# Dividing a gate-and-up tile over two blocks of the 23rd and 24th attention units, in place of the last down tile

## The chip, the cores and the metric

The kernel runs on one NeuronCore of a Trainium2 chip. The metric is the device time of one execution in microseconds (us). Before the change three runs took 1396.32, 1397.09 and 1397.90 us; their median is 1397.09 us. "TensorE" or PE is the matmul engine, PEld its weight loads, ScalarE or ACT the activation engine, VectorE or DVE the elementwise engine, GpSimd or POOL and SyncE or SP the two others; SP and POOL issue most DMAs.

## What is computed

A layer norm of 2048 tokens of 512 features feeds an attention of 32 heads of 16 features, and beside it a SwiGLU feed-forward of width 1792, whose output gates the attention's:

```python
xn = _layernorm(x, axis=-1)
s = _A_ref(xn, A_wqkv, A_wo)        # softmax(q k' / 4) v, 32 heads of 16, then @ wo
g = _silu(_B_ref(xn, B_w_gate, B_w_up, B_w_down))   # (silu(xn@w_gate) * (xn@w_up)) @ w_down
return x + s * g
```

Shapes: x is [1, 2048, 512], `wqkv` [512, 1536], `wo` [512, 512], `w_gate` and `w_up` [512, 1792], `w_down` [1792, 512], all float32.

## The kernel before

**Units and blocks.** After a prologue (layer norm, projections to q, k, v) attention runs in 32 *units*: 8 groups of 4 heads times 4 batches of 512 queries (`units`, line 463). A unit goes over its 2048 keys in 16 *key tiles* of 128. It is cut into three *blocks* of 4 to 6 key tiles, so there are 96 blocks, numbered 0 to 95 here; unit *u*, counted from 0, has blocks 3*u* to 3*u*+2. The 23rd and 24th units are thus blocks 66 to 71, the 29th and 30th are blocks 84 to 89. `run(u, first, n)` (line 963) issues one block of *n* key tiles.

**What a block does.** It has 2*n* *score pairs*: for each key tile two pairs of heads, each pair two matmuls that run side by side on the two halves of TensorE's rows. Most pairs are *direct* (`scored`, line 950): they go into one of two double banks `score0` and `score1`, and ScalarE's exponential (line 954) reads the bank and writes a `pr` tile. The others are *copied* (lines 1001 to 1017): they go half by half into the spare bank `acc1`, VectorE copies them out, and ScalarE takes their exponential in place afterwards (line 1024). At the end come the *values*: for each key tile eight matmuls (line 409) that multiply `pr` by v into `acc0`, for all 128 rows of TensorE.

**The fillers.** While ScalarE works through the scores, TensorE is given other work, in *filler pairs*: two matmuls, again one on each half of the rows, into `bankx` and `banky` (`both`, line 185, and lines 379 to 380). They come from generators in a queue: `ffn(b)` for the four batches of tokens, then the output projections `project_out`. A feed-forward batch has two groups of 7 gate-and-up tiles (24 pairs each) followed by 4 down tiles (21 pairs each). At the end of a gate-and-up tile ScalarE takes a tanh of `bankx` (line 239) and VectorE makes the hidden tile from both banks (lines 240 to 241); at the end of a down tile of the second group VectorE adds the banks to `y` and ScalarE takes a tanh of `y` (line 191).

**How many fillers a block gets** stands in the list `sizes` (lines 483 to 492), one number a block, and so one tile a block. There are 88 feed-forward tiles, of which the first is done in the prologue, and the projections make 8 entries more; that is 95 for 96 blocks. One tile is therefore divided over two blocks. Before the change it is the last down tile: 11 pairs in block 86 and 10 in block 87. Block 88 (`early`) has the first part of the projection (18 pairs), block 89 and those after it 24 each, but 12 in blocks 92 and 93.

**Order within a block.** `events(n, f, ahead)` (line 511) sets how many pairs are direct and lays direct scores (D), halves of copied ones (A, B) and fillers (F) out in a row. VectorE's other work waits in the list `chores` and is let in between the copies where it has room. What a unit leaves to do when its values are complete (`finish`, line 437: transposing `acc0`, scaling) joins that list behind the first two scores of the next unit.

**Begun blocks.** Where the next block's number is in `begins` (line 493), `run` issues the next block's first two direct scores ahead of the last key tile's values (lines 1031 to 1034), so that ScalarE has work during them. Before, blocks 86, 87, 88, 92 and 93 are begun in this way. Lines 496 to 509 set the number of key tiles: 4, 6, 6 or 6, 6, 4 in the last four units, elsewhere 5, 5, 5 with one more in one block.

**The end of the feed-forward.** After each down tile of the last batch `next_out` (line 284) splits a piece of `wo` and of the attention output for the projection, and loads the next piece of `wo` into one buffer (`wor`). Block 88 needs the first three of them, block 89 the fourth.

Of the kernel before, what the change touches and what calls it, by code (L numbers as in the profile page):

```python
# [39 lines left out]
DC = D // HALF  # L40
# [3 lines left out]
EPS = 1e-5  # L44
TURNS = (0, 0, 0, 0, 0, 2, 4, 6, 8, 10, 13, 16, 16)
COPIES = ((0, 0, 0, 1, 1, 1, 1, 0, 0, 0, 0, 2), (1, 1, 0, 0, 1, 1, 1, 1, 2, 2, 0, 0))
QSLOT = (0, 1, 0)
KSLOT = (0, 0, 1)

# [2 lines left out]
def tile_block(ctx: ExitStack, tc: tile.TileContext, x, wqkv, wo, w_gate, w_up, w_down, out):  # L52
# [42 lines left out]
    def load_rows(dst, src, slots):  # L95
        for h in range(2):
            for s, part in enumerate(slots):
                r = h * HALF + 2 + s * DH
                sp.dma_start(dst[r:r + DH].bitcast(F32),
                             src[part].rearrange("(j h d) t -> h d j t", j=2, h=2)[h])  # L100
# [5 lines left out]
    def load_q(u, i=None):  # L106
        g, b = divmod(u, NB)
        load_rows(qst[u % 2 if i is None else i], q_d[:, g * 64:(g + 1) * 64, b * TB:(b + 1) * TB], QSLOT)

# [353 lines left out]
    units = NG * NB  # L463
# [19 lines left out]
    sizes = []  # L483
    for _ in range(NB):
        for part in GROUPS:
            nf = part.stop - part.start
            sizes += [3 * DC] * nf + [3 * nf] * NT
    split = sizes[-1] // 2
    sizes = sizes[1:-1] + [sizes[-1] - split, split]
    early = len(sizes)  # L490
    pair = 6 * DT
    sizes += [6 * (DT - 1), pair, pair, pair, pair // 2, pair // 2, pair, pair]
    begins = (early - 2, early - 1, early, early + 4, early + 5)

    blocks, opened = [], []
    for u in range(units):
        opened.append(len(blocks))
        if u == 0:
            ns = [4, 6, 6]
        elif u >= units - 4:  # L500
            ns = ([4, 6, 6] if u % 2 else [6, 6, 4])
        else:
            ns = [5] * 3
            far = sizes[len(blocks):len(blocks) + 3]
            ns[far.index(max(far)) if far[1] < max(far) else 1] = 6
        kt = 0
        for n in ns:
            blocks.append((u, kt, n))
            kt += n
# [23 lines left out]
    with ExitStack() as pro:  # L533
# [119 lines left out]
        def split_x(b, t, av, between=None):  # L653
            hi, lo = (xt[b % 2][j][:, :, t * P:(t + 1) * P] for j in range(2))
            nc.scalar.copy(hi, av)
            if between:
                between()
            dve.tensor_sub(lo, av, hi.bitcast(F32))
# [119 lines left out]
        def copy_fx(i):  # L778
            i, w = divmod(i, 2)
            i, u = divmod(i, 2)  # L780
            j, h = divmod(i, 2)
            dst = fx[halves[h], j].rearrange("p (c u) t -> u p c t", u=2)[u]
            nc.scalar.copy(dst[:, 2 * w:2 * w + 2], xt[0][j][halves[u], 2 * w:2 * w + 2])
# [13 lines left out]
        for b in range(NB):  # L797
# [3 lines left out]
            for n, (make, i) in enumerate(slots):  # L801
# [27 lines left out]
                if b == 0 and n == 2:  # L829
                    split_x(0, 0, xf)  # L830
                for _ in range(COPIES[b][n] if b < 2 else 0):
                    copy_fx(copied.pop(0))
# [57 lines left out]
        with tc.If(fast < 1):  # L890
            with tc.tile_pool(name="gen", bufs=1) as gen:
                for h in range(2):
                    pool.memset(qst[0][h * HALF:h * HALF + 2].bitcast(F32), 0.0)
                for g in range(NG):
                    for b in range(NB):
                        u = g * NB + b
# [244 lines left out]
```

## Time and profile before

| what | value |
| --- | --- |
| median of three runs | 1397.09 us |
| the profiled execution's own time | 1397.09 us |
| its span, first to last instruction | 1395.3 us |
| TensorE matmuls busy | 1387.7 us, 99% of the span |
| weight loads busy | 849.8 us, 61% |
| ScalarE busy | 1087.4 us, 78% |
| VectorE busy | 755.9 us, 54% |
| mean DMA rate | 106 GB/s |

The profile is one execution. "Busy" adds up the time in which at least one instruction of an engine is running; matmuls overlap in the pipeline, so 99% for TensorE doesn't say that it runs as densely as it can. In a row of the trace's list in order of time, the first number is the start, the second the length, both in us; instructions of one kind that follow each other are merged ("x48" is 48 matmuls), and what stands in brackets is the engine's idle time before it and what ended it. The 8 matmuls of each key tile at line 409 make these rows a ruler: a block ends where its last row of values ends, which is start plus length.

### The profile page before, as it was taken

To read this page: it belongs to the slowest core of one execution; us is meant where nothing else is said; L and a number is where in the kernel's file an instruction comes from. 1 tells how busy PE (TensorE), PEld (TensorE's weight loads), DVE (VectorE), ACT (ScalarE), POOL (GpSimd) and SP (SyncE) were. 2 spreads that over 40 slices of the span, in tenths; PEclk is the share of its full clock that TensorE was granted. 3 is DMA by queue.
4 is the path that set the end of the run, shared out by engine and by line. 5 is a ranking of instruction groups with operands and counts; after the bars stand their busy time and mean duration, and the time that the engine had idled before them with its cause. 6 is when DMAs were issued, how large, how long until landed. Compare 5 with 4: busy or idle time off the path is not lost.

```text
span 1395.3 us, 27643 instructions
## 1 busy us (share of the span) xinstructions
PE 1387.7 (99%) x11193; PEld 849.8 (61%) x11193; DVE 755.9 (54%) x1293; ACT 1087.4 (78%) x1245; POOL 73.7 (5%) x92
## 2 busy tenths in 40 slices
PE   9999999999999999999999999999999999999998
PEld 7777755655665565565556556655655665564555
DVE  6674555455645653556456645654565445555544
ACT  6753678877888877787888778778877877889785
POOL 4200200000000000000000000000000000000222
PEclk9999999999999999999999999999999999999999
DMA  7778641043534511154514303256134113234323
GB/s 228 271 246 267 173 107 43 14 115 85 130 86 118 119 43 36 51 132 97 136 53 110 97 13 73 74 141 149 57 76 114 32 47 80 63 92 141 116 86 137
DMA packets 126953, 148.13 MB, mean 106 GB/s; under 512 B 12524, under 2 KB 79340, under 8 KB 126052
## 3 DMA queue, kind: packets, MB, share of 16 engines
q1 hardware_dynamic: 121620, 125.79, 34.8%
q0 software_dynamic: 4912, 20.12, 3.9%
q8 instruction: 89, 1.46, 0.4%
q14 instruction: 44, 0.36, 0.1%
q10 hardware_dynamic: 288, 0.39, 0.1%
HBM read 106.68 MB, written 39.58 MB: 105 GB/s over the span
## 4 chain that ended last, share of the span: by engine, by line
PE 88%; ACT 0%; DVE 0%; issue 0%; DVEq 0%
PE acc L409 32%; PE bankx L187 23%; PE score L948 17%; PE banky L187 10%; PE acc L948 3%; PE bankx L380 2%; PE banky L380 1%; ACT pr L954 0%; PE acc L1078 0%; PE bankx L1078 0%; PE score L1078 0%; DVE pr L1010 0%; DVE y L1085 0%; DVE pr L1016 0%; DVE fx L1022 0%
## 5 line engine op out<-in xcount | busy, mean ns | idle before, releaser
L954 ACT ACTIVATE pr<-score 128x1024 f32<-128x1024 f32 x860 | 813.4, 1032 | 226.2 <-PE score L948 224.5
L409 PE MATMUL acc<-pr,vst 128*17 128x512 f32 x4096 | 459.1, 593 | 0.0
L948 PE MATMUL score<-qst,kst 50*128 50x512 f32 x1720 | 395.4, 412 | 0.1
L187 PE MATMUL bankx<-fx,guh 64*128 64x512 f32 x896 | 333.5, 393 | 0.1
L187 PE MATMUL banky<-fx,guh 64*128 64x512 f32 x896 | 324.9, 393 | 0.0
L409 PEld LDWEIGHTS acc<-pr,vst 128*17 128x17 f32 x4096 | 109.9, 97 | 290.6 <-issue 270.9
L948 PEld LDWEIGHTS score<-qst,kst 50*128 50x128 f32 x1720 | 176.3, 184 | 142.5 <-issue 66.3
L1010 DVE COPY pr<-acc 128x512 f32<-128x512 f32 x164 | 113.3, 691 | 188.1 <-PE acc L948 186.0
L187 PE MATMUL bankx<-wd,hh 64*128 64x512 f32 x672 | 201.2, 392 | 0.0
L187 PE MATMUL banky<-wd,hh 64*128 64x512 f32 x672 | 198.8, 393 | 0.0
L187 PEld LDWEIGHTS bankx<-fx,guh 64*128 64x128 f32 x896 | 166.6, 186 | 18.4 <-issue 0.9
L187 PE MATMUL banky<-fx,gul 64*128 64x512 f32 x448 | 175.6, 392 | 0.0
L187 PE MATMUL bankx<-fx,gul 64*128 64x512 f32 x448 | 175.4, 392 | 0.0
L187 PEld LDWEIGHTS banky<-fx,guh 64*128 64x128 f32 x896 | 166.5, 186 | 5.5
L1024 ACT ACTIVATE pr<-pr 128x1024 f32<-128x1024 f32 x164 | 168.0, 1078 | 0.0
L1016 DVE COPY pr<-acc 128x512 f32<-128x512 f32 x164 | 113.3, 691 | 74.9 <-PE acc L948 65.9
L240 DVE SCALAR_TENSOR_TENSOR ga<-th,bankx 128x512 f32<-128x512 f32 x56 | 38.5, 688 | 177.9 <-ACT th L239 177.9
L187 PEld LDWEIGHTS bankx<-wd,hh 64*128 64x128 f32 x672 | 124.9, 186 | 14.2 <-DVE fx L1022 0.8
L948 PE MATMUL acc<-qst,kst 50*128 50x512 f32 x328 | 131.9, 402 | 0.1
L187 PEld LDWEIGHTS banky<-wd,hh 64*128 64x128 f32 x672 | 124.5, 186 | 3.5
L187 PEld LDWEIGHTS bankx<-fx,gul 64*128 64x128 f32 x448 | 83.7, 187 | 9.9
L187 PEld LDWEIGHTS banky<-fx,gul 64*128 64x128 f32 x448 | 83.6, 186 | 3.2
(186 smaller groups left out, 1296.3 us busy)
## 6 DMA issues: line engine op xcount, KB each, us to landing
gur<-in_B_w_gate_dram SPq DMA_DIRECT2D x56, 256.0 KB
gur<-in_B_w_up_dram SPq DMA_DIRECT2D x56, 256.0 KB
wdr<-in_B_w_down_dram SPq DMA_DIRECT2D x56, 256.0 KB
kst<-k_d SPq DMA_DIRECT2D x192, 64.0 KB
qst<-q_d SPq DMA_DIRECT2D x192, 64.0 KB
fx<-xt_d SPq DMA_DIRECT2D x24, 512.0 KB
q_d<-parts SPq DMA_DIRECT2D x16, 512.0 KB
k_d<-parts SPq DMA_DIRECT2D x16, 512.0 KB
```

Of the source, the lines that this page charges most:

```text
L187: mm(banks[i], lhs[halves[i]], rhs[halves[i]], start=start, stop=stop)
L240: dve.scalar_tensor_tensor(ga, th, 1.0, bankx, op0=ALU.add, op1=ALU.mult)
L380: mm(banks[k], lhs[b, c][a][halves[h], (j + k) * P:(j + k + 1) * P], fx[halves[h], w, c], start=swap == i == 0, stop=i == 3 * n - 1, skip_ ...
L409: mm(acc[0][h * 32:h * 32 + DH + 1], v[:, kt % CT, h * (DH + 1):(h + 1) * (DH + 1)], probs[kt, h // 2][:, h % 2], start=kt == 0, stop=kt = ...
L948: mm(bank, k[r, j, kc * P:(kc + 1) * P], qst[u % 2][r, j], start=True, stop=True)
L954: act(pr, score[slot], AF.Exp, scale=0.25)
L1010: dve.tensor_copy(probs[kt, j][:, 0], spare_bank)
L1016: dve.tensor_copy(probs[kt, j][:, 1], spare_bank)
L1024: act(probs[kt, j], probs[kt, j], AF.Exp, scale=0.25)
```

## The change

One table entry is added and three rules of the plan are written anew. Nothing else differs; all lines behind the first stand one line lower.

```diff
+PARTED = (22, 23)
...
-    split = sizes[-1] // 2
-    sizes = sizes[1:-1] + [sizes[-1] - split, split]
+    sizes = sizes[1:]
+    sizes[3 * PARTED[0] + 2:3 * PARTED[1]] = [3 * DC // 2] * 2
     early = len(sizes)
     pair = 6 * DT
     sizes += [6 * (DT - 1), pair, pair, pair, pair // 2, pair // 2, pair, pair]
-    begins = (early - 2, early - 1, early, early + 4, early + 5)
+    begins = tuple(3 * u + i for a in (PARTED[0], units - 2) for u, i in ((a, 2), (a + 1, 0)))
 
     blocks, opened = [], []
     for u in range(units):
         opened.append(len(blocks))
         if u == 0:
             ns = [4, 6, 6]
-        elif u >= units - 4:
+        elif u in PARTED or u >= units - 2:
             ns = ([4, 6, 6] if u % 2 else [6, 6, 4])
         else:
             ns = [5] * 3
```

The gate-and-up tile that block 68 had whole is now 12 pairs in block 68 and 12 in block 69. Every tile behind it comes one block later, up to the last down tile, which block 87 now has whole. Blocks 68, 69, 92 and 93 are begun; 86, 87 and 88 no longer are. By the plan:

| block | before: key tiles, fillers, begun | after: key tiles, fillers, begun |
| --- | --- | --- |
| 66, 67, 68 (23rd unit) | 5, 24 / 6, 24 / 5, 24 | 6, 24 / 6, 24 / 4, 12, begun |
| 69, 70, 71 (24th) | 5, 24 / 6, 24 / 5, 24 | 4, 12, begun / 6, 24 / 6, 24 |
| 72, 73, 74 | 5, 21 / 6, 21 / 5, 21 | 6, 24 / 5, 21 / 5, 21 |
| 75, 76, 77 | 5, 21 / 6, 24 / 5, 24 | 5, 21 / 5, 21 / 6, 24 |
| 78, 79, 80 | 5, 24 / 6, 24 / 5, 24 | 5, 24 / 6, 24 / 5, 24 |
| 81, 82, 83 | 5, 24 / 6, 24 / 5, 21 | 5, 24 / 6, 24 / 5, 24 |
| 84, 85, 86 (29th) | 6, 21 / 6, 21 / 4, 11, begun | 5, 21 / 6, 21 / 5, 21 |
| 87, 88, 89 (30th) | 4, 10, begun / 6, 18, begun / 6, 24 | 5, 21 / 5, 18 / 6, 24 |

In the 29th and 30th units this makes 21+21+21 and 21+18+24 filler pairs, 63 in each, where it was 53 and 52.

**TensorE, the end of block 68 and the start of block 69.** `acc_80` is `acc0`, where the values go, `acc_81` the spare bank; a row "x2" is one pair of scores. Before:

```order
L187 MATMUL bankx<-fx,gul 128x512
L187 MATMUL banky<-fx,gul 128x512
L409 MATMUL acc_80<-pr,vst_8976 17x512 x4
L409 MATMUL acc_80<-pr,vst_8980 17x512 x16
L948 MATMUL score_8970<-qst_8987,kst_549 128x512 x2
L948 MATMUL score_8971<-qst_8987,kst_549 128x512 x2
L187 MATMUL bankx<-fx,guh 128x512
L187 MATMUL banky<-fx,guh 128x512
L948 MATMUL acc_81<-qst_8987,kst_553 128x512
```

After:

```order
L188 MATMUL bankx<-fx,gul 128x512
L188 MATMUL banky<-fx,gul 128x512
L949 MATMUL score_8970<-qst_557,kst_8979 128x512 x2
L410 MATMUL acc_80<-pr,vst_8980 17x512 x12
L949 MATMUL score_8970<-qst_8987,kst_549 128x512 x2
L949 MATMUL score_8971<-qst_8987,kst_549 128x512 x2
L410 MATMUL acc_80<-pr,vst_8980 17x512 x4
L188 MATMUL bankx<-fx,guh 128x512
L188 MATMUL banky<-fx,guh 128x512
L949 MATMUL score_8970<-qst_8987,kst_549 128x512 x2
```

The next unit's first two score pairs now stand ahead of the last key tile's values, and the fillers behind them go on with the same gate-and-up tile.

**TensorE, the end of block 87 and the start of block 88**, where the projection begins (line 380). Before:

```order
L948 MATMUL score_8970<-qst_8987,kst_8979 128x512 x2
L409 MATMUL acc_80<-pr,vst_8980 17x512 x12
L948 MATMUL score_8970<-qst_8987,kst_8983 128x512 x2
L948 MATMUL score_8971<-qst_8987,kst_8983 128x512 x2
L409 MATMUL acc_80<-pr,vst_8980 17x512 x4
L380 MATMUL bankx<-fx,part 128x512
L380 MATMUL banky<-fx,part 128x512
L948 MATMUL score_8970<-qst_8987,kst_8983 128x512 x2
L948 MATMUL acc_81<-qst_8987,kst_549 128x512
```

After:

```order
L188 MATMUL bankx<-wd,hh 128x512
L188 MATMUL banky<-wd,hh 128x512
L410 MATMUL acc_80<-pr,vst_8980 17x512 x16
L410 MATMUL acc_80<-pr,vst_8984 17x512 x4
L949 MATMUL score_8970<-qst_8987,kst_8983 128x512 x2
L949 MATMUL score_8971<-qst_8987,kst_8983 128x512 x2
L381 MATMUL bankx<-fx,part 128x512
L381 MATMUL banky<-fx,part 128x512
L949 MATMUL acc_81<-qst_8987,kst_549 128x512
```

Block 88's first two score pairs now stand behind all of block 87's values.

**VectorE from the end of block 85 (before) or 86 (after) into block 87.** `fx<-wor` and `part<-pair` are `next_out`'s splits, `o<-acc_80` the transposition that frees the value bank. Before:

```order
L1022 CAST fx<-wor 128x512
L1010 COPY pr<-acc_81 128x512
L1016 COPY pr<-acc_81 128x512
L1022 TENSOR_TENSOR fx<-wor,fx 128x512
L1022 CAST part<-pair 128x512
L1022 TENSOR_TENSOR part<-pair,part 128x512
L420 STREAM_TRANSPOSE o<-acc_80 128x512
L425 RECIPROCAL rl<-o 128x16
L1010 COPY pr<-acc_81 128x512
```

After:

```order
L1023 CAST fx<-wor 128x512
L1023 TENSOR_TENSOR fx<-wor,fx 128x512
L1011 COPY pr<-acc_81 128x512
L1023 CAST part<-pair 128x512
L1017 COPY pr<-acc_81 128x512
L1023 TENSOR_TENSOR part<-pair,part 128x512
L1011 COPY pr<-acc_81 128x512
L421 STREAM_TRANSPOSE o<-acc_80 128x512
L426 RECIPROCAL rl<-o 128x16
```

The third `next_out` (first row here) has moved from block 86 into block 87, the transposition still stands behind it, with three copies in between where there were two.

## The prediction

> **What bounds the kernel now.** I read the page first, then the list in order of time, where the rows of values mark the blocks, then the waits of the blocks that change.
>
> ```profile
> span 1395.3 us, 27643 instructions
> PE 1387.7 (99%) x11193; PEld 849.8 (61%) x11193; DVE 755.9 (54%) x1293; ACT 1087.4 (78%) x1245; POOL 73.7 (5%) x92
> ```
>
> TensorE is busy from end to end, so a gain can only come from blocks in which its busy time is stretched. To find these, I take the block ends around the 23rd unit (start plus length of each row of values):
>
> ```profile
> 997.52 5.34 PE L409 MATMUL acc<-pr,vst 128*17 128x512 f32 x48
> 1010.99 4.49 PE L409 MATMUL acc<-pr,vst 128*17 128x512 f32 x40
> 1024.08 5.34 PE L409 MATMUL acc<-pr,vst 128*17 128x512 f32 x48
> ...
> 1088.71 4.49 PE L409 MATMUL acc<-pr,vst 128*17 128x512 f32 x40
> 1101.50 5.34 PE L409 MATMUL acc<-pr,vst 128*17 128x512 f32 x48
> 1114.28 4.49 PE L409 MATMUL acc<-pr,vst 128*17 128x512 f32 x40
> ```
>
> Block 65 ends at 1002.86, block 66 (5 key tiles, 24 fillers) at 1015.48, block 67 (6, 24) at 1029.42: 12.62 and 13.94 us. Blocks 72 to 74 end at 1093.20, 1106.84 and 1118.77: block 74 (5, 21) takes 11.93 us. From these three forms follows a line: 1.32 us for a key tile (13.94 - 12.62), 0.23 for a filler pair ((12.62 - 11.93) / 3), and 12.62 - 5 x 1.32 - 24 x 0.23 = 0.50 us for a block's two turns between scores and values. Block 73 (6, 21) should take 13.25 and takes 13.64: 0.39 over. Now the end of the feed-forward:
>
> ```profile
> 1230.59 4.49 PE L409 MATMUL acc<-pr,vst 128*17 128x512 f32 x40
> 1243.24 5.34 PE L409 MATMUL acc<-pr,vst 128*17 128x512 f32 x48
> 1256.74 4.49 PE L409 MATMUL acc<-pr,vst 128*17 128x512 f32 x40
> 1261.81 1.05 PE L409 MATMUL acc<-pr,vst 128*17 128x512 f32 x8
> 1267.35 2.77 PE L409 MATMUL acc<-pr,vst 128*17 128x512 f32 x24
> 1270.71 1.05 PE L409 MATMUL acc<-pr,vst 128*17 128x512 f32 x8
> 1276.30 2.77 PE L409 MATMUL acc<-pr,vst 128*17 128x512 f32 x24
> 1279.67 1.05 PE L409 MATMUL acc<-pr,vst 128*17 128x512 f32 x8
> 1288.93 5.34 PE L409 MATMUL acc<-pr,vst 128*17 128x512 f32 x48
> 1303.11 5.34 PE L409 MATMUL acc<-pr,vst 128*17 128x512 f32 x48
> ```
>
> An x8 row behind a longer one shows a begun block: the last key tile's values stand alone, behind the next block's first scores. Blocks 83 to 89 end at 1235.08, 1248.58, 1262.86, 1271.76, 1280.72, 1294.27 and 1308.45. Against the line, block 84 (6, 21) takes 13.50 for 13.25, block 85 (6, 21) 14.28 for 13.25, block 86 (4, 11) 8.90 for 8.31, block 87 (4, 10) 8.96 for 8.08, block 88 (6, 18) 13.55 for 12.56, block 89 (6, 24) 14.18 for 13.94: over by 0.25, 1.03, 0.59, 0.88, 0.99 and 0.24, together 3.98 us. What stretches 86 to 88, in the waits of TensorE's weight loads from 1262.86 to 1294.27:
>
> ```profile
> PEld score L948 <- ACT pr L1024: 1.7, 2, 0.9
> PEld acc L948 <- DVE pr L1010: 1.4, 4, 0.5
> PEld score L948 <- ACT pr L954: 0.7, 2, 0.4
> ```
>
> These loads wait for exponentials and for copies of the spare bank: with 10, 11 or 18 fillers there isn't enough other work between the scores.
>
> **The change part by part.** Blocks 66 to 89 hold 128 key tiles and 522 filler pairs in both kernels, in 24 blocks. The line gives them the same time, so the change is worth what it does to the time over the line. Before, that is 3.98 and block 73's 0.39: 4.37 us.
>
> *Blocks 67 to 69 take on the divided tile and two begins.* The nearest rows are blocks 91 to 93, of the same 6, 4 and 4 key tiles and 24, 12 and 12 fillers:
>
> ```profile
> 1317.35 5.34 PE L409 MATMUL acc<-pr,vst 128*17 128x512 f32 x48
> 1331.59 4.49 PE L409 MATMUL acc<-pr,vst 128*17 128x512 f32 x40
> 1336.67 1.05 PE L409 MATMUL acc<-pr,vst 128*17 128x512 f32 x8
> 1342.24 2.77 PE L409 MATMUL acc<-pr,vst 128*17 128x512 f32 x24
> 1345.60 1.05 PE L409 MATMUL acc<-pr,vst 128*17 128x512 f32 x8
> 1351.17 3.63 PE L409 MATMUL acc<-pr,vst 128*17 128x512 f32 x32
> ```
>
> Ends 1322.69, 1337.72, 1346.65 and 1354.80: 15.03, 8.93 and 8.15 us against 13.94, 8.54 and 8.54. Block 93 is short because its first scores were paid in 92. The sum over the line is 1.09; block 91 is a projection block, and these lie 0.24 over without any begin (block 89), so the begins and the division cost 0.85. One thing differs: a gate-and-up tile ends in block 69, with a tanh.
>
> ```profile
> 997.80 0.62 ACT L239 ACTIVATE th<-bankx 128x512 f32<-128x512 f32 x1
> 998.28 1.06 ACT L954 ACTIVATE pr<-score 128x1024 f32<-128x1024 f32 x1
> ...
> 1352.26 1.05 ACT L1024 ACTIVATE pr<-pr 128x1024 f32<-128x1024 f32 x1
> ```
>
> It delays what follows on ScalarE by 0.48 us (997.80 to 998.28). In block 93 ScalarE's last exponential ended at 1353.31, and the last key tile's values, which need it, began three key tiles of 0.85 us (5.34 - 4.49) after 1351.17, at 1353.72. So 0.41 of the 0.48 is hidden; I put 0.1, the bounds being 0 and 0.48. The lower bound of the whole is 0.85 less block 92's 0.39 = 0.46, if the projection's own turn-over of the banks lies in it. The upper bound is that these blocks cost what 85 to 87 did, 1.03 + 0.59 + 0.88 = 2.50, and 0.48: 2.98. I take 0.85 + 0.1 = 0.95, because 12 fillers stand between the scores as in 92 and 93, not 10 or 11.
>
> A begin adds one turn from values to half-row scores and one back. What a turn looks like in the weight loads, at the start of block 88's begun scores:
>
> ```profile
> 1278.03 0.12 PEld L409 LDWEIGHTS acc<-pr,vst 128*17 128x17 f32 x4 [0.31 <-issue]
> 1279.00 0.30 PEld L948 LDWEIGHTS score<-qst,kst 50*128 50x128 f32 x4 [0.85 <-ACT pr L1024]
> ```
>
> The loads stand idle for 0.85 us at the turn instead of the 0.31 between values. The Trainium skill has the rule for it (TensorEngine Tiling (Array Packing), Key Properties): a change of tiling mode drains TensorE. The idle time agrees with it; by the rule alone the change would keep two of the three begins' price, and the sum would be rival two's 1395.5 us.
>
> *Blocks 70 to 84 shift.* They become ordinary forms, (6, 24), (5, 24) and (5, 21), on the line; no 6-by-21 block is left among them, which removes 73's 0.39 and 84's 0.25. Nothing on them is on another path: the weights of a gate-and-up tile are issued two tiles ahead as before.
>
> *Block 85* (6, 21) is what 84 was: 0.25. *86 and 87* (5, 21) are on the line. *Block 88* (5, 18), not begun, is a form that the trace lacks. Its direct scores stand four slots apart, as in (5, 21), which shows no stall; it has the projection's wait for the turned-over banks, which I price by block 89 at 0.24. Bounds: 0, and the 0.99 of the begun block 88. *Block 89* keeps its 0.24. One more pair is copied (165 for 164): two VectorE copies, under TensorE's fillers with VectorE at 54%; without that cover they would cost the spare bank's wait, 1.4 / 4 = 0.35 us each.
>
> In block 87 the value bank's transposition now stands behind `next_out` and three copies. Block 84 has that order in the trace:
>
> ```profile
> 1239.48 0.70 DVE L420 STREAM_TRANSPOSE o<-acc 128x512 f32<-128x512 f32 x1
> ```
>
> It ends 3.1 us before that block's values begin (1243.24). With two copied pairs instead of three, block 87's third copy stands about 2 slots later, and with one key tile less its values begin 2 slots earlier: 4 x 0.23 = 0.9 us, so 2.2 are left, and I cost it at nothing.
>
> Sum over the line after: 0.95 + 0.25 + 0.24 + 0.24 = 1.68. The gain is 4.37 - 1.68 = 2.69 us. The profiled execution's own time is 1397.09 us, of which 1.79 lie outside its span, and it equals the median of the three runs: 1397.09 - 2.69 = **1394.4 us**. With all unknowns at their low ends (0.46, 0 for block 88) the gain is 3.42, 1393.7; with the high ones (2.98, 0.99) it is -0.09.
>
> **The rivals.** *One: the stretch is denser than my line says.* Weight loads per time, in the 23rd, 29th and 30th units and blocks 91 to 93:
>
> ```profile
> 1002.86:1042.02 39.16, 39.16 (x339) 23.09 (x338) 23.57 (x39) 31.35 (x35) 0.54 (x1) 1.00 0.32 78
> 1235.08:1271.76 36.68, 36.68 (x304) 20.87 (x304) 19.91 (x34) 32.59 (x36) 1.21 (x3) 1.00 0.19 59
> 1271.76:1308.45 36.69, 36.21 (x295) 20.20 (x294) 19.98 (x37) 30.02 (x32) 3.94 (x5) 1.00 0.37 123
> 1322.69:1354.80 32.11, 32.11 (x267) 18.58 (x266) 15.28 (x30) 26.62 (x28) 4.99 (x6) 1.00 0.26 83
> ```
>
> PEld (third figure) is 59.0% of the 23rd unit, but 56.9 and 55.1% of the 29th and 30th. At 59.0% those 41.07 us of loads take 69.6 instead of 73.4, a gain of 3.8; blocks like 91 to 93 (57.9%) give back 32.11 - 18.58 / 0.59 = 0.6. Gain 3.2: 1393.9 us. Against it: block 88's turn-over stays. The Trainium skill (Perfetto Trace Analysis, Identifying the Most-Contended Engine) judges TensorE by this share and not by matmul busy time; here the latter reads 100% in three of the four rows.
>
> *Two: the excess goes with the begins.* Blocks 85 to 88 have 3.49 us over the line and three begins, 1.16 each; one begin fewer and block 73 gain 1.16 + 0.39 = 1.55, 1395.5 us. Against it: blocks 91 to 93 have two begins and 0.85 in all.
>
> *Three: ScalarE decides the divided blocks* as it did 85 to 87, and block 88 is paced by its exponentials (half of its 0.99). For it: the waits above, and the tanh. After: 2.50 + 0.25 + 0.5 + 0.24 = 3.49, gain 0.9: 1396.2 us. Against it: 12 fillers take 0.23 to 0.46 us more of TensorE than 11 and 10.
>
> *Four, slower: `wo` comes late.* One buffer takes the next piece of `wo` in turn; the load is issued behind a split and needed at the head of VectorE's next block, where copies and transposition queue behind it, and TensorE behind the spare bank.
>
> ```profile
> 1251.63 0.68 DVE L1022 TENSOR_TENSOR part<-pair,part 128x512 fp32r<-128x512 f32 x1
> 1261.78 0.42 DVE L1022 CAST fx<-wor 128x512 fp32r<-128x512 f32 x1
> o_d<-o POOLq DMA_DIRECT2D x12, 256.0 KB, 2.5
> ```
>
> Before, 9.5 us lay between (1252.31 to 1261.78, in block 85's 14.28); in 11.93-us blocks it is 7.1. It decides from a landing of 7.1 us; at 8.6 three loads would cost 4.5 us, and the time is 1398.9. Against it: 256 KB land in 2.5 us in the row above.
>
> **How the numbers follow.** My forecast 0.55, rival one 0.23, two 0.06, three 0.09, four 0.07. About 0.2% (2.8 us) is what a measurement of this kernel can tell from no change, so faster means below 1394.3: just under my sum. The forecast, whose own range is 1393.7 to 1395.2, gives 0.29 to faster and 0.26 to within; rival one is faster, two and three within, four slower: 0.52, 0.41, 0.07. The range goes from 1393.3 (the low ends and half a microsecond for the runs' scatter) to 1396.6, which takes in rival three.
>
> **What would show it.** Block lengths in the rows of values: 67 to 69 at about 14.7, 8.9 and 8.3 us, 86 and 87 at 11.9 each, 88 at 11.5; the stretch from the end of 65 to the end of 89 at 302.9 instead of 305.59. The waits of score loads for `pr` in 86 to 88 should fall to those of an ordinary block. If 68 and 69 take over 9 us each, or 88 over 12, rival three holds; an idle VectorE ahead of `fx<-wor` shows rival four. The prediction is wrong if anything outside 66 to 89 changes its length.

## The result, and the profile after

The changed kernel takes 1394.30 us (median of 17 runs, 1393.72 to 1395.10), the one before 1397.04 us (17 runs, 1396.32 to 1397.90): a ratio of 0.998, 95% interval 0.9973 to 0.9987. It is faster by 2.74 us, 0.2%. The profiled execution took 1393.72 us, the shortest of the 17.

The first rows of its page, and its rows of values (start and length in us; a block ends at their sum, as in the prediction):

```profile
span 1391.9 us, 27644 instructions
PE 1385.1 (100%) x11193; PEld 847.3 (61%) x11193; DVE 757.7 (54%) x1295; ACT 1087.3 (78%) x1245; POOL 73.8 (5%) x92
```

```profile
997.12 5.34 PE L410 MATMUL acc<-pr,vst 128*17 128x512 f32 x48
1011.11 5.34 PE L410 MATMUL acc<-pr,vst 128*17 128x512 f32 x48
1025.09 4.49 PE L410 MATMUL acc<-pr,vst 128*17 128x512 f32 x40
1030.17 1.05 PE L410 MATMUL acc<-pr,vst 128*17 128x512 f32 x8
1035.65 2.77 PE L410 MATMUL acc<-pr,vst 128*17 128x512 f32 x24
1039.02 1.05 PE L410 MATMUL acc<-pr,vst 128*17 128x512 f32 x8
1044.58 3.69 PE L410 MATMUL acc<-pr,vst 128*17 128x512 f32 x32
...
1225.79 4.49 PE L410 MATMUL acc<-pr,vst 128*17 128x512 f32 x40
1237.74 4.49 PE L410 MATMUL acc<-pr,vst 128*17 128x512 f32 x40
1250.39 5.34 PE L410 MATMUL acc<-pr,vst 128*17 128x512 f32 x48
1263.18 4.49 PE L410 MATMUL acc<-pr,vst 128*17 128x512 f32 x40
1275.10 4.49 PE L410 MATMUL acc<-pr,vst 128*17 128x512 f32 x40
1286.53 4.49 PE L410 MATMUL acc<-pr,vst 128*17 128x512 f32 x40
1299.84 5.34 PE L410 MATMUL acc<-pr,vst 128*17 128x512 f32 x48
```

Blocks 65 to 69 end at 1002.46, 1016.45, 1031.22, 1040.07 and 1048.27: 66 to 69 take 13.99, 14.77, 8.85 and 8.20 us. Blocks 83 to 89 end at 1230.28, 1242.23, 1255.73, 1267.67, 1279.59, 1291.02 and 1305.18: 84 to 89 take 11.95, 13.50, 11.94, 11.92, 11.43 and 14.16. From the end of 65 to the end of 89 pass 302.72 us instead of 305.59, so 2.87 us came from this stretch. The span is shorter by 3.4; 0.4 of that lies ahead of block 66, which the change doesn't touch, and 0.1 behind block 89. The end of block 65 moves that much between executions (1002.46 to 1003.25 in the profiles of the runs that leave the blocks ahead of it alone), and none of the blocks 1 to 65 and 90 to 95 changed by more than 0.07 us.

| piece | over the line, before | forecast after | after |
| --- | --- | --- | --- |
| 67 to 69 | 0 | 0.95 | 0.83 + 0.31 - 0.34 = 0.80 |
| 73, 84 (6 key tiles, 21 fillers before) | 0.39 + 0.25 | 0 | 0 |
| 85 | 1.03 | 0.25 | 0.25 |
| 86, 87 | 0.59 + 0.88 | 0 | 0.00 |
| 88 | 0.99 | 0.24 | 0.19 |
| 89 | 0.24 | 0.24 | 0.22 |
| sum | 4.37 | 1.68 | 1.46 |

What TensorE's weight loads wait for in blocks 86 to 88 (1255.74 to 1291.02; total, times, longest in us), which answers to the waits shown of before:

```profile
PEld score L949 <- issue: 3.4, 4, 0.9
PEld score L949 <- ACT pr L955: 0.7, 4, 0.2
```

The wait for the spare bank's copies (1.4 us before) is gone. The waits for ScalarE's score banks are where they were, 0.7, but block 73, which lies on the line, shows 0.4 by itself. The four "<- issue" are the turns from values to half-row scores at the starts of blocks 86 to 89, 0.85 us each. The 1.7 us "<- ACT pr L1024" of before have the same length, 0.85 us each, and stand at the same kind of turn. So they need not be waits for exponentials, as I had read them; the fourth experiment decides it.

### The profile page after: what moved, and what is told of

The parts are those of the page before. It is cut to its first block, busy times and chain, and to the rows that moved or that the text cites. A ratio compares the mean times of both kernels' runs of the same rounds, so it can differ in the third digit from the quotient of the medians.

```text
span 1391.9 us, 27644 instructions
## 1 busy us (share of the span) xinstructions
PE 1385.1 (100%) x11193; PEld 847.3 (61%) x11193; DVE 757.7 (54%) x1295; ACT 1087.3 (78%) x1245; POOL 73.8 (5%) x92
## 3 DMA queue, kind: packets, MB, share of 16 engines
q8 instruction: 89, 1.46, 0.4%
## 4 chain that ended last, share of the span: by engine, by line
PE 88%; ACT 0%; DVE 0%; issue 0%; DVEq 0%
PE acc L410 32%; PE bankx L188 23%; PE score L949 17%; PE banky L188 9%; PE acc L949 3%; PE bankx L381 2%; PE banky L381 1%; ACT pr L955 0%; PE acc L1079 0%; PE bankx L1079 0%; PE score L1079 0%; DVE y L1086 0%; DVE y L1092 0%; DVEq L1138 0%
## 5 line engine op out<-in xcount | busy, mean ns | idle before, releaser
L955 ACT ACTIVATE pr<-score 128x1024 f32<-128x1024 f32 x859 | 812.7, 1032 | 223.1 <-PE score L949 221.3
```

What stands on the lines that cost most here:

```text
L955: act(pr, score[slot], AF.Exp, scale=0.25)
```

## The experiments

All were timed against the kernel before on the same chip. Block lengths come from their rows of values, read as above, with 0.01 us of rounding, and from one profile each; blocks that an edit leaves alone mostly agree between these profiles within 0.1 us. Where the interval of a ratio holds 1, the whole time tells nothing, and only the blocks are evidence.

**Begins taken out of the new plan.**

```diff
-    begins = tuple(3 * u + i for a in (PARTED[0], units - 2) for u, i in ((a, 2), (a + 1, 0)))
+    begins = (early + 4, early + 5)
```

> The new plan, with blocks 68 and 69 no longer begun. Theory (short of other work, TensorE waits for ScalarE, and a begin shortens that wait for two turns of about 0.4 us together): block 67 falls from 14.77 to 13.95 us, but 68 and 69 each start with a cold ScalarE. In 68, 6 direct exponentials (0.63 + 6 x 0.96) and 2 copied ones (1.95) end 8.3 us after the block's start, and the last key tile's values could begin at 7.6: 8.54 + 0.75 = 9.3 us; 69 has a tanh more, 9.8. Blocks 67 to 69 take 33.0 instead of 31.81, the kernel 1395.5 us. Rival (the time over the line goes with the begins): 67 to 69 fall to the line, 31.0 us, the kernel 1393.5.

Measured: 1396.08 us, ratio 0.9992 (0.9983 to 1.0001). Blocks 67, 68 and 69 took 13.96, 9.21 and 10.12 us, together 33.29 instead of 31.82. TensorE's weight loads from 1030 to 1057 show where it went:

```profile
PEld acc L410 <- ACT pr L1025: 2.8, 4, 1.2
```

The values wait for the last exponentials of copied scores. A begin costs its two turns, but in a block of 12 fillers it saves more.

**Begins taken out of the old plan.**

```diff
-    begins = (early - 2, early - 1, early, early + 4, early + 5)
+    begins = (early + 4, early + 5)
```

> The kernel before, with blocks 86, 87 and 88 no longer begun. Theory: 85 falls to 13.5 us, 86 and 87 wait for ScalarE's last exponentials and take 9.3 each, 88 13.4; together 45.5 instead of 45.69, no change of the whole within 0.5 us (1397). Rival (the 3.49 us over the line in 85 to 88 go with the three begins): these blocks fall to about 42.4, the kernel to 1393.7.

Measured: 1397.08 us, ratio 1.0 (0.9991 to 1.0009). Blocks 85 to 88 took 13.50, 9.40, 9.24 and 13.48, together 45.62 for 45.69. The excess doesn't go with the begins; rival two of the prediction falls. What comes in their place stands in the waits of the weight loads from 1261.97 to 1294.09:

```profile
PEld acc L409 <- ACT pr L1024: 1.7, 5, 0.5
PEld score L948 <- ACT pr L954: 1.4, 3, 0.6
```

Without a begin the values wait for ScalarE, 1.7 us of a kind that the list of before doesn't have.

**The division alone.** As in the first experiment, and the 23rd and 24th units cut 5, 6, 5:

```diff
-        elif u in PARTED or u >= units - 2:
+        elif u >= units - 2:
```

> The new plan's division alone: blocks 68 and 69 have 12 fillers each, but 5 key tiles and no begin, and the 23rd and 24th units are cut 5, 6, 5. Theory: 8 direct exponentials stand 4 slots apart where only 12 fillers are left to stand between them, so TensorE waits: 68 takes about 11.7 and 69 12.2 us where the line has 9.86; blocks 66 to 71 take 77.1 instead of 73.7, and the gain is gone: 1397.7 us. Rival (begins are what costs): no begin, so these blocks fall to the line, 72.8, and the kernel to 1393.4.

Measured: 1397.59 us, ratio 1.0004 (0.9995 to 1.0013). Block 68 took 11.21 us and 69 13.43. In 69 the row of values itself is stretched, 6.18 us for five key tiles that take 4.49 elsewhere, and the score loads wait for ScalarE from 1030 to 1057:

```profile
1048.04 6.18 PE L410 MATMUL acc<-pr,vst 128*17 128x512 f32 x40
```

```profile
PEld score L949 <- ACT pr L955: 3.4, 5, 1.2
```

Moving the divided tile gains nothing by itself. With five key tiles and 12 fillers ScalarE decides, if these waits are right; its work was not halved in this run. The short blocks and the begins around it are what makes it cheap.

**Is it ScalarE in blocks 86 to 88?** The kernel before, with half the exponentials there:

```diff
+HALVED = (86, 88)
...
-        act(pr, score[slot], AF.Exp, scale=0.25)
+        if HALVED[0] <= now + ahead <= HALVED[1]:
+            pool.memset(pr[:, 1], 1.0)
+            act(pr[:, 0], score[slot][:, 0], AF.Exp, scale=0.25)
+        else:
+            act(pr, score[slot], AF.Exp, scale=0.25)
...
-            act(probs[kt, j], probs[kt, j], AF.Exp, scale=0.25)
+            part = slice(0, 1 if HALVED[0] <= now <= HALVED[1] else 2)
+            act(probs[kt, j][:, part], probs[kt, j][:, part], AF.Exp, scale=0.25)
```

> The kernel before, where in blocks 86 to 88 ScalarE takes the exponential of the first head of each pair alone; GpSimd writes ones for the second head of a direct pair, and that of a copied pair stays as copied, so half of the softmax numerators of these blocks are left out. Theory (ScalarE stretches 86 to 88): with half of its work the blocks fall to the line but for the turns, 85 to 88 together from 45.69 to about 43.4 us, the kernel to 1394.8. Rival (the begins' turns stretch them): 45.7, no change, 1397.0.

Measured: 1396.98 us, ratio 0.9999 (0.9990 to 1.0008). My expectation was wrong. The exponentials did shrink:

```profile
L957 ACT ACTIVATE pr<-score 128x512 f32<-128x512 f32 x23 | 13.3, 597 | 11.6 <-PE score L949 8.5 <-POOL pr L956 1.6 <-PE acc L949 1.0
```

23 of them at 597 ns, and ScalarE now idle mostly for TensorE's scores. But 85 to 88 took 14.27, 8.84, 8.67 and 13.71, together 45.49: 0.20 less. The loads' 0.7 us for ScalarE's score banks is gone from their list, and the three gaps of about 0.85 us ahead of score loads stay, now with other labels:

```profile
PEld score L949 <- issue: 1.7, 2, 0.8
PEld score L949 <- ACT th L192: 0.9, 1, 0.9
```

A gap that keeps its length, whatever its label names, is a turn and not a wait for exponentials. ScalarE was not what stretched these blocks. (GpSimd's constants delayed a few exponentials, 1.6 us in all; the scores' banks were still free earlier.)

**Or the spare bank?** In the order of time of the kernel before, VectorE's work ahead of the turn-over of the banks in block 88, and the weight load behind it:

```profile
1283.54 0.68 DVE L1022 TENSOR_TENSOR fx<-wor,fx 128x512 fp32r<-128x512 f32 x1
1284.21 0.69 DVE L1010 COPY pr<-acc 128x512 f32<-128x512 f32 x1
1284.82 0.14 DVE L384 COPY turned_over<-bankx 1x1 f32<-1x1 f32 x1
1285.01 0.18 PEld L380 LDWEIGHTS bankx<-fx,part 64*128 64x128 f32 x1 [0.81 <-DVE turned_over L384]
```

The small copies that must see the banks before TensorE may go on stand behind a copy of 0.69 us, itself behind a split of `wo`, and TensorE's loads idle for 0.81. So the second theory: VectorE's copies of the spare bank.

```diff
+HALVED = (86, 88)
...
+    def spare_copy(dst):
+        cut = TB // 2 if HALVED[0] <= now <= HALVED[1] else TB
+        dve.tensor_copy(dst[:, :cut], spare_bank[:, :cut])
+        if cut < TB:
+            pool.memset(dst[:, cut:], 0.0)
...
-                dve.tensor_copy(probs[kt, j][:, 0], spare_bank)
+                spare_copy(probs[kt, j][:, 0])
...
-                dve.tensor_copy(probs[kt, j][:, 1], spare_bank)
+                spare_copy(probs[kt, j][:, 1])
```

> The kernel before, where in blocks 86 to 88 VectorE copies only the first half of each spare bank, GpSimd writes zeros for the rest, so half of the copied scores of these blocks (an eighth to a quarter of all) is left out. Theory, new after the halved exponentials changed nothing: beside 0.40 us for each begin, TensorE waits in these blocks for the spare bank, whose two halves stand 5.6 to 6 filler slots apart while matmul, copy and two signals take longer. With the copies cut from 0.69 to about 0.37 us, 86 falls from 8.90 by 0.2, 87 from 8.95 by 0.2, 88 from 13.56 by 0.5 to 0.7 (its turn-over of the banks also stands behind a copy): 85 to 88 from 45.69 to about 44.7, the kernel to 1396.1. Rivals (ScalarE decides; or the begins alone): no change of these blocks, 1397.1.

Measured: 1396.42 us; the ratio, 0.9996 (0.9987 to 1.0005), can't tell 0.6 us from nothing, but the blocks can. Its rows of values for 85 to 88:

```profile
1262.17 1.05 PE L410 MATMUL acc<-pr,vst 128*17 128x512 f32 x8
1267.61 2.77 PE L410 MATMUL acc<-pr,vst 128*17 128x512 f32 x24
1270.97 1.05 PE L410 MATMUL acc<-pr,vst 128*17 128x512 f32 x8
1276.28 2.77 PE L410 MATMUL acc<-pr,vst 128*17 128x512 f32 x24
1279.64 1.05 PE L410 MATMUL acc<-pr,vst 128*17 128x512 f32 x8
1288.11 5.34 PE L410 MATMUL acc<-pr,vst 128*17 128x512 f32 x48
```

Blocks 85 to 88 end at 1263.22, 1272.02, 1280.69 and 1293.45: 86 takes 8.80, 87 8.67 and 88 12.76 (8.90, 8.96 and 13.55 before). With 85 at 14.30 that is 44.53, 1.16 less, 0.79 of it in block 88. The waits of block 88's weight loads that end on VectorE's banks show where, before and with half copies:

```profile
PEld bankx L380 <- DVE turned_over L384: 0.8, 1, 0.8
PEld acc L948 <- DVE pr L1010: 0.8, 2, 0.5
```

```profile
PEld bankx L381 <- DVE turned_over L385: 0.5, 1, 0.5
PEld acc L949 <- DVE pr L960: 0.3, 1, 0.3
```

By these lists the turn-over's wait is 0.3 shorter and the spare bank's 0.5, together what the block lost. The split of `wo` is as long as it was, so what it adds to the turn-over's wait is still in the 0.5 that is left; no run moves it alone.

**Both halved.** The two edits together.

> The kernel before with both in blocks 86 to 88: half of the exponentials and half of VectorE's copies, so half of the numerators and half of the copied scores of these blocks are left out or replaced by constants. Theory (0.40 us a begin, the rest waits for the spare bank, of which ScalarE has a small share): the blocks keep the begins' 1.2 us and come close to the line otherwise, 85 to 88 at 44.0 to 44.4 (half copies alone: 44.54), the kernel at about 1395.9. If ScalarE and the copies hide each other's waits, it falls further, below 43.7; if the begins cost all that is left, 44.5.

Measured: 1396.17 us, ratio 0.9992 (0.9983 to 1.0001); 14.29, 8.59, 8.40 and 12.91, together 44.19, as the theory had it. Of the 3.49 us over the line in 85 to 88, 1.50 go when both engines' work is halved: 1.16 with VectorE's alone, 0.20 with ScalarE's alone, 0.14 more with both. What is left is 1.99 (44.19 less the line's 42.20). Of this, 1.2 are an estimate for the three begins, at the 0.40 that blocks 67 to 69 of the changed kernel pay for each of two; no run measures a begin in blocks 86 and 87 alone. Another 0.49 is an estimate of what is there without begins too: 0.25 as in block 84 and 0.24 as in the projection's block 89. The last 0.3 no run places; half of each engine's work is also still there.

**Block 88 begun again in the new plan.**

```diff
-    begins = tuple(3 * u + i for a in (PARTED[0], units - 2) for u, i in ((a, 2), (a + 1, 0)))
+    begins = (early,) + tuple(3 * u + i for a in (PARTED[0], units - 2) for u, i in ((a, 2), (a + 1, 0)))
```

> The changed kernel with block 88 begun as it was before, but not 86 and 87. Blocks 87 and 88 take 11.92 + 11.43 = 23.35 us in the changed kernel. Theory (a begin 0.40, and in a begun block 88 the small copies that read the turned-over banks fall behind a VectorE copy of the spare bank): 0.40 + 0.36 + up to 0.2 more, 24.1 to 24.3, the kernel 1395.2. Rival (the begin alone): 23.75, 1394.7. Rival (the fewer waits of 88 came from its five key tiles, not from the begin taken away): 23.35, 1394.3.

Measured: 1395.41 us, ratio 0.9988 (0.9979 to 0.9997). Blocks 87 and 88 took 12.69 and 11.78, 24.47: 1.12 more than the 23.35 without the begin, somewhat beyond the expected 0.75 to 0.95. The wait at the turn-over is back with its 0.8 us, so a begin of this block is dear with five key tiles too, and it was not the sixth key tile alone that made the old block 88 long. But the sixth key tile isn't cheap either. In the run of the old plan without begins, block 88 (6 key tiles, 18 fillers) took 13.48, 0.92 over the line, with waits of 0.8 us for the spare bank's copies and none for the turn-over; with five key tiles and no begin it is 0.19 over. The changed plan took both away.

**How few fillers will do.**

```diff
-    sizes[3 * PARTED[0] + 2:3 * PARTED[1]] = [3 * DC // 2] * 2
+    sizes[3 * PARTED[0] + 2:3 * PARTED[1]] = [14, 10]
```

> The changed kernel with the tile divided 14 and 10 instead of 12 and 12. The line (0.23 us a filler pair, whatever the block) says 68 at 9.30, 69 at 7.74, their sum unchanged, 1394.3. Theory that a block of 4 key tiles has a floor under ScalarE's 7 direct exponentials, one copied and a tanh (8.2 us): 69 stays at 8.1, the sum grows by 0.36, 1394.7.

Measured: 1394.73 us, ratio 0.9985 (0.9976 to 0.9994). 68 took 9.21, 69 8.46, 17.67 instead of 17.05: 0.62 more, where the line has none and I expected 0.36. With 10 fillers and a tanh, block 69 is longer than with 12. Its weight loads have waits that block 69 of the changed kernel lacks: 0.5 us for ScalarE ahead of the values, and one each for a score bank and for the spare bank:

```profile
PEld score L949 <- ACT pr L955: 0.4, 1, 0.4
PEld acc L949 <- DVE pr L1011: 0.4, 1, 0.4
```

The second comes from the plan. `events` counts whole slots for fillers and direct scores and half a slot for a half of a copied score. In a begun block of 4 key tiles it sets the two halves 5.5 slots apart with 12 fillers, but 4.5 with 11 or 10. The wait stands in the blocks of 11 and 10 fillers, 86 and 87 of the kernel before (0.3 us each) and 69 here, and in none of those with 12 (68, 69 and 92). Here the line ends; whether ScalarE or the spare bank ends it, this run doesn't show.

**Another tile divided.** The tile over blocks 74 and 75, a down tile far from the projection:

```diff
-PARTED = (22, 23)
+PARTED = (24, 25)
...
-    sizes[3 * PARTED[0] + 2:3 * PARTED[1]] = [3 * DC // 2] * 2
+    sizes[3 * PARTED[0] + 2:3 * PARTED[1]] = [11, 10]
```

> The changed plan with another tile divided: a down tile of the first group (11 and 10 fillers) over blocks 74 and 75 of the 25th and 26th units, far from the projection, instead of the gate-and-up tile in 68 and 69. Theory (few fillers and the 6-by-21 blocks beside them cost, wherever they stand): against the changed kernel 0.33 us for each of three more blocks of 6 key tiles and 21 fillers, 0.2 for 74 and 0.45 for 75, 1.6 in all: 1395.9 us. Rival (what costs is the neighbourhood of block 88 alone): only the three blocks, 1395.3. Rival (dividing a down tile costs what it did at the end): 1397.

Measured: 1396.06 us, ratio 0.9990 (0.9981 to 0.9999). The stretch 66 to 89 took 304.41 us, 1.69 more than in the changed kernel: 72 to 76 took 13.50, 14.44, 8.98, 8.16 and 13.63 us. The three blocks of 6 key tiles and 21 fillers are 0.25, 1.19 (with a begin) and 0.38 over, 74 (11 fillers, begun) 0.67, 75 (10) 0.08. Far from block 88 a divided down tile gains 1.2 us on the kernel before (1397.24 on the same chip), the gate-and-up tile 2.7. So the place counts, and so does the kind of tile: this one brings 11 and 10 fillers, with the same spare-bank wait of 0.4 us in each block, and three blocks of 6 key tiles and 21 fillers beside it.

**The spare bank in the ordinary blocks.** If its copies cost TensorE in 86 to 88, they may do so in the blocks of 6 key tiles and 21 fillers, which were over the line from the start. VectorE in block 85 of the changed kernel:

```profile
1247.48 0.69 DVE L1017 COPY pr<-acc 128x512 f32<-128x512 f32 x1 [0.84 <-PE acc L949]
1248.76 0.69 DVE L1011 COPY pr<-acc 128x512 f32<-128x512 f32 x1 [0.59 <-PE acc L949]
1250.04 0.69 DVE L1017 COPY pr<-acc 128x512 f32<-128x512 f32 x1 [0.58 <-PE acc L949]
```

Where copies follow each other as fast as they can, they start 1.28 us apart: 0.69 for the copy and 0.59 until the next half has been computed. That is 5.6 slots of 0.23 us. The plan asks for 5.6, but `events` rounds: in these blocks the six halves stand 5.5, 5.5, 6.5, 4.5 and 5.5 slots apart. The 4.5, 1.04 us, is less than the round trip, and TensorE's weight loads wait there, once in the block:

```profile
PEld acc L949 <- DVE pr L1017: 0.3, 1, 0.3
```

The edit asks for 6, which comes out as 5.5 or 6.5 throughout:

```diff
-        marks += [((0.3 if ahead else 2.2) + max(5.6, min(8, (length - 5) / (2 * copied))) * i, "AB"[i % 2]) for i in range(2 * copied)]
+        marks += [((0.3 if ahead else 2.2) + max(6.0, min(8, (length - 5) / (2 * copied))) * i, "AB"[i % 2]) for i in range(2 * copied)]
```

> The changed kernel with the halves of the copied scores at least 6.0 instead of 5.6 filler slots apart. This moves instructions in the five blocks of 6 key tiles and 21 fillers (7, 19, 40, 52, 85) and a little in 88. Theory (these blocks lie 0.25 to 0.39 us over the line because a half of a copied score waits for VectorE's copy of the half before): each falls by 0.2 to 0.3, the kernel by 1.0 to 1.5 us, to about 1393. Rival (they are over the line because of their three exponentials of copied scores at the end): later copies make them longer, by about 0.1 each, 1394.8.

Measured: 1393.66 us, ratio 0.9975 (0.9966 to 0.9984). The five blocks (7, 19, 40, 52 and 85) took 13.40, 13.33, 13.33, 13.39 and 13.31 for 13.65, 13.48, 13.47, 13.62 and 13.50: 0.96 less. But block 88 grew from 11.43 to 11.89. So the last version keeps 5.6 there (`max(5.6 if now == early else 6.0, ...)`):

> The changed kernel with the halves of copied scores 6.0 filler slots apart in the five blocks of 6 key tiles and 21 fillers, and block 88 left as it was, where 6.0 had put the turn-over behind a copy (11.43 to 11.89 us). Theory: the five blocks keep the 1.04 us that they gained with 6.0, 88 stays at 11.43: 1394.3 - 1.04 = 1393.3 us, faster than both kernels. Rival (the gain of those blocks is scatter): 1394.3.

Measured: 1393.11 us (median of 7), ratio 0.997 (0.9959 to 0.9982): the lowest median of all. Its interval overlaps those of the run before and of the changed kernel, so the blocks are the evidence: the five took 13.40, 13.34, 13.33, 13.41 and 13.31, block 88 11.43. VectorE in its block 85, in the same place as above:

```profile
1247.23 0.69 DVE L1017 COPY pr<-acc 128x512 f32<-128x512 f32 x1 [0.59 <-PE acc L949]
1248.79 0.69 DVE L1011 COPY pr<-acc 128x512 f32<-128x512 f32 x1 [0.87 <-PE acc L949]
1250.08 0.69 DVE L1017 COPY pr<-acc 128x512 f32<-128x512 f32 x1 [0.59 <-PE acc L949]
```

A copy that followed after 1.28 us now follows after 1.56, and the wait of 0.3 us is gone from the list of this block. One thing in this expectation was wrong, as block 88 shows in the trace with 6.0 everywhere:

```profile
1282.47 0.15 DVE L385 COPY turned_over<-bankx 1x1 f32<-1x1 f32 x1 [0.36 <-PE bankx L381]
1283.54 0.69 DVE L1011 COPY pr<-acc 128x512 f32<-128x512 f32 x1 [0.81 <-PE acc L949]
```

The turn-over did not fall behind a copy; VectorE was idle ahead of it. A half of a copied score had moved from ahead of the turn-over's wait to behind it, where it no longer covers that wait. Block 88 then shows waits that the changed kernel's doesn't: 0.3 us for a score bank, 0.3 for exponentials ahead of the values, 0.3 for the spare bank and 0.2 at the turn-over. Which of them make up the 0.46, twice a slot, is open.

## Why the prediction was right, and where not

- *The line.* Right: equal numbers of key tiles, fillers and blocks are worth the same time, and the blocks that only changed their form came out on it (86 and 87 at 11.94 and 11.92, forecast 11.9). Nothing outside blocks 66 to 89 changed by more than 0.07 us. The line holds for forms that the trace shows undisturbed; with few fillers it ends.
- *Blocks 67 to 69.* Forecast 0.95 over the line, measured 0.80. The tanh hardly shows: block 69 took 8.20, block 93 without one 8.15. Taking blocks 91 to 93 as the model rather than 85 to 87 was the choice that mattered. Its reason, that 12 fillers stand between the scores instead of 10 or 11, holds: 12 keep the halves of a copied score apart by more than 4.5 slots.
- *Block 88* without a begin: 0.24 forecast, 0.19 measured. The size was right, but the reason given for it, a wait for the turned-over banks, isn't shown: the weight loads of blocks 88 and 89 list no such wait after the change. That it came so close is in part luck, and where the 0.2 us of these blocks comes from is open. *Block 87's* transposition cost nothing, as forecast; nor did `wo`: VectorE took the split of the last piece without an idle time ahead of it, so rival four falls:

```profile
1278.46 0.69 DVE L193 SCALAR_TENSOR_TENSOR y<-th,y 128x512 f32<-128x512 f32 x1 [0.75 <-ACT th L192]
1279.07 0.42 DVE L1023 CAST fx<-wor 128x512 fp32r<-128x512 f32 x1
```

- *The sum.* 2.69 us forecast, 2.87 in the trace's stretch, 2.74 between the medians. The whole time alone can't tell my forecast from rival one's 1393.9; the shares below do.
- *The step that failed* is the reading of the waits: "these loads wait for exponentials and for copies of the spare bank: with 10, 11 or 18 fillers there isn't enough other work between the scores". Half of the exponentials changed 0.20 us there, and the 1.7 us that I read as waits for them were turns. The copies of the spare bank do count: half of them changed 1.16, by the lists 0.3 of it at the turn-over of block 88, which my three lines of waits left out. So the excess of 85 to 88 was VectorE's copies and the turn-over behind one, the begins (1.2 us by the estimate above), and a small share of ScalarE. The lack of fillers acts in part through the spacing of the copied halves. The sum didn't depend on this reading, because the excess was measured as a whole and the new forms were priced from rows of the same form; only block 88's form was new.
- *Rival one* (loads per time) gave 3.2 us. The shares after show why it is a poor price. Weight loads are the third figure of each row, for the 23rd, 29th and 30th units:

```profile
1002.47:1040.08 37.61, 37.61 (x318) 21.51 (x318) 22.34 (x37) 32.30 (x36) 0.54 (x1) 1.00 0.31 79
1230.28:1267.67 37.39, 37.39 (x320) 22.75 (x320) 22.68 (x38) 31.84 (x35) 1.53 (x3) 1.00 0.25 73
1267.67:1305.19 37.52, 37.52 (x321) 22.90 (x320) 21.56 (x40) 30.90 (x33) 4.04 (x6) 1.00 0.39 134
```

  The 29th and 30th units rose from 56.9 and 55.1 to 60.8 and 61.0%, above the 59.0% that I took as their limit, and the 23rd fell to 57.2%. Two units with at most 0.3 us over the line, the 23rd before (72 fillers) and the 29th after (63), show 59.0 and 60.8%: the share moves with what a unit holds, not with its waits alone.
- *Rivals two and three* fell with the runs above: begins are worth their price where fillers are few, and only without them do the waits point to ScalarE (10.12 us for a block 69 that is not begun, 13.43 with five key tiles).

## What to carry to other kernels

Where a loop's steps come in a few forms, a line through three undisturbed forms prices a plan made of such forms, and what lies over the line is what a change of plan can win; here it came within 0.2 us of the measured gain. A form that the trace lacks can lie over the line, as the blocks with few fillers did. A list of waits names who came last, not what it costs: halve the suspect's work before believing it. A copy out of a bank that is filled again at once has a round trip; a spacing that equals it on paper falls below it once rounded to slots, and costs a wait each time (0.3 us here).

## What the runs showed of the hardware

- The spare bank's round trip, matmul to copy to matmul to copy, takes 1.28 us with a copy of 0.69 us; 0.36 us of it is neither the copy nor TensorE's 0.23 us for a slot.
- A turn from values to half-row scores leaves the weight loads idle for 0.85 us; halving ScalarE's work left it as it was.
- Halved work isn't half the time. Exponentials and copies, groups of the kernel before (first two rows) and copies of the run with half copies:

```profile
L954 ACT ACTIVATE pr<-score 128x1024 f32<-128x1024 f32 x860 | 813.4, 1032 | 226.2 <-PE score L948 224.5
L1010 DVE COPY pr<-acc 128x512 f32<-128x512 f32 x164 | 113.3, 691 | 188.1 <-PE acc L948 186.0
```

```profile
L960 DVE COPY pr<-acc 128x256 f32<-128x256 f32 x10 | 4.2, 419 | 7.5 <-PE acc L949 7.5
```

  From 1024 to 512 columns an exponential goes from 1032 to 597 ns, from 512 to 256 columns a copy from 691 to 419 ns: both keep a fixed part of about 0.15 us, if the rest goes with the columns (2 x 597 - 1032 = 162, 2 x 419 - 691 = 147 ns).
